# One batch's k^T v steps half a unit later, and one expert's row gathers after the first results

## The chip, the cores and the metric

The kernel runs on one core of a Trainium2 chip. A core has five engines with a queue of instructions each: TensorE (PE; its weight loads are listed as PEld) multiplies matrices into PSUM, VectorE (DVE) and ScalarE (ACT) work on rows, GpSimd (POOL) does small vector work and issues the indirect DMAs, SyncE (SP) issues plain DMAs. Engines wait for each other through semaphores. The metric is the device time of one execution in microseconds (us), and a lower time is better.

## The reference

The computation is linear attention followed by a mixture of experts. The 8 batches have 576 tokens and 8 heads of 64 columns each.

```python
kv = np.einsum('bhsd,bhse->bhde', k, v)
out = np.einsum('bhsd,bhde->bhse', q, kv)
rms = np.sqrt(np.mean(out * out, axis=-1, keepdims=True) + 1e-06)
x = (out / rms * g_norm)              # then (B,H,S,D) -> (4608, 512)
do_compute = x @ w_skip > 0           # the other tokens are passed through
logits = xc @ w_gate                  # xc: the computed tokens; 8 experts
e_idx = np.argmax(logits, axis=1)     # gate_w: softmax at e_idx
h = np.maximum(xc[mask] @ w1[e], 0.0) # 512 -> 1024, tokens of expert e
y[mask] = gate_w[mask, None] * (h @ w2[e])
out[do_compute] = xc + y
```

## The kernel before

Everything is written in one order by hand; the framework adds the semaphores from what the instructions read and write, but moves nothing.

**Attention.** A *unit* `n` is the work on two tiles of 128 tokens for four of the eight heads, and there are 36 of them. A batch has nine chunks of 64 tokens; two pairs of units (`i` = 0 and 1) take eight of these, so a batch has four units. The ninth chunks, the *last tokens*, of four batches are gathered into a pair of units of their own, for which `i` is `None`: units 16 and 17 for the first four batches, 34 and 35 for the others. The fifth batch (b = 4) begins at unit 18. In step `n` of the main loop come, in this order: `turn(n + 1)` (PE transposes q, L460, ACT copies it), `root(n - 1)` (ACT, L525), the jobs listed under "early", `values(n)` (PE multiplies q with k^T v, L496, or L504 for the last tokens; ACT squares, L510), `norm(n - 1)` (DVE reciprocal L532 and scaling `xl`, L537), `squares(n)` (DVE sum, L518; later units have these two the other way round), then the jobs listed under "pe". The values of a unit go to one of two PSUM buffers `o_ps`, which DVE's `xl` frees. The units with `i` = 0 also copy the last tokens of q aside (L479).

A batch's k^T v is summed on PE in portions (`state`, L379), which are spread over the "pe" slots of earlier steps by the table `portions`. After the last portion ACT copies the sum into the tile `kvd` (L386), and three more jobs follow: the *turn* `state_t` (PE turns k^T v by a product with the identity, L393, ACT copies it to `kvT`, L396), the *gate products* `state_m` (PE multiplies `kvT` with the gate's weights, L402, ACT copies two small blocks, L405) and the *exchange* `state_s` (PE moves the halves to the other partitions, L411, ACT copies them, L415). Their PSUM bank `g_ps` is also that of the ranks (`rank`, L645 to L651), which number the tokens within their expert.

**Experts.** Each expert has a fixed number of slots, in the order of their token counts; r = 0 is the fullest. The x rows were written to `out` in DRAM; `gather_all(r, ...)` fetches an expert's rows to a tile `xg` with one indirect DMA per piece (POOL, L1084), `enter` transposes them (PE, L1093), `layer_1` or `fast_1` and `layer_2` or `fast_2` are the two products (PE, L1112, L1124 and L1192), and `result` adds gate times product to the rows (DVE, L1336) and scatters them into `out` (POOL, L1339). As gathers and scatters touch the same DRAM tensor, a gather waits for all scatters ahead of it in the program to have landed, and a scatter for all gathers ahead of it. `blank` clears unused columns of the next hidden tile (POOL, L1106). The weights come by SP (L336 and L346), when PE has finished with the tile that they replace. Expert 0 has its first 192 rows done early, its `result` for these stands in two pieces before its other work. The tiles `xg` of the other experts have three buffers, so that those of experts 1, 2 and 3 are free from the start.

Two places matter here. In the loop over batches that lists the jobs, with `step` the step after the last portion; for the fifth batch `step` is 16, and for it these are the last lines:

```python
at(step, "early", lambda b=b: state_t(b))
at(step, "pe", lambda b=b: state_m(b))
at(step + 1, "early" if step + 1 == n else "pe", lambda b=b: state_s(b))
```

And the gathers of the first three experts (r = 0, 1, 2), which stand together as soon as the slots' rows are known; in `experts`, each later expert r issues those of r + 2 at its start.

Of the kernel before, what the change touches and what calls it, by code (L numbers as in the profile page):

```python
# [17 lines left out]
def kernel(  # L18
# [117 lines left out]
    def load_q(b):  # L136
        if b < B:
            qts[b] = load(q_pool, "q", q, b)
# [93 lines left out]
    for a in range(2):  # L232
        r = slice(a * 64, (a + 1) * 64)
# [45 lines left out]
    for r, cap in enumerate(ROOMS):  # L279
        pieces, off = [], 0  # L280
# [74 lines left out]
    def own(b, w):  # L355

        return kvds[b % KVD][w * 64:(w + 1) * 64, :, w, w, :]
# [7 lines left out]
    def ends_of(x):  # L365

        ap = [list(d) for d in x.ap]
        assert ap[-1] == [1, PK]
        return bass.AP(x.tensor, x.offset, ap[:-1] + [[PK - G, 2], [1, G]])

    def state(b, some):

        kt, vt = kts[b], vts[b]
        for i in some:
            u, c = divmod(i, C)
            for w in range(2):
                for a in range(2):
                    r = slice(a * 64, (a + 1) * 64)
                    nc.tensor.matmul(  # L379
                        out=sum_ps[w * 64:(w + 1) * 64, a, u, :],  # L380
                        lhsT=kt[r, 2 * u + w, c, :], rhs=vt[r, 2 * u + w, c, :],
                        start=(c == 0), stop=(c == C - 1), skip_group_check=True)
        if some.stop < 2 * C:
            return
        for w in range(2):
            nc.scalar.copy(out=own(b, w)[:, :, G:G + 2 * D].rearrange("p u (a d) -> p a u d", a=2),  # L386
                           in_=sum_ps[w * 64:(w + 1) * 64, :, :, :])

    def state_t(b):
        for u in range(2):  # L390
            for w in range(2):
                r = slice(w * 64, (w + 1) * 64)
                nc.tensor.matmul(out=kvT_ps[:, u, r], lhsT=kvds[b % KVD][:, u, w, w, G:G + 2 * D],  # L393
                                 rhs=ident[:, r], start=True, stop=True)
        kvT = att_pool.tile([P, 2, P], FP32, tag="kvT", name="kvT", bufs=1)
        nc.scalar.copy(out=kvT[:, :, :], in_=kvT_ps)  # L396
        kvTs[b] = kvT

    def state_m(b):
        kvT = kvTs.pop(b)  # L400
        for u in range(2):
            nc.tensor.matmul(out=lg_ps[:, u, :, :, :], lhsT=kvT[:, u, :], rhs=gw_b[:, u, :, :, :],  # L402
                             start=True, stop=True)
        for w in range(2):
            nc.scalar.copy(out=ends_of(own(b, w)), in_=lg_ps[w * 64:(w + 1) * 64, :, :, w, :])  # L405

    def state_s(b):

        for w in range(2):
            r, o = slice(w * 64, (w + 1) * 64), slice((1 - w) * 64, (2 - w) * 64)  # L410
            nc.tensor.matmul(out=sw_ps[o, :], lhsT=ident[r, r], rhs=own(b, w), start=True, stop=True,  # L411
                             skip_group_check=True)
        for w in range(2):
            o = slice((1 - w) * 64, (2 - w) * 64)
            nc.scalar.copy(out=kvds[b % KVD][o, :, w, 1 - w, :],  # L415
                           in_=sw_ps[o, :].rearrange("p (u k) -> p u k", u=2))


    units = []
# [22 lines left out]
    def at(step, part, job):  # L442
        todo.setdefault((step, part), []).append(job)
# [470 lines left out]
    for b, n in starts.items():  # L914
        if b:
            step, counts = portions[b]
            i = 0
            for count in counts:
                at(step, "pe", lambda b=b, some=range(i, i + count): state(b, some))
                i += count  # L920
                step += 1
            assert i == 2 * C and step < n and step - len(counts) > over - 1
            at(step, "early", lambda b=b: state_t(b))
            at(step, "pe", lambda b=b: state_m(b))
            at(step + 1, "early" if step + 1 == n else "pe", lambda b=b: state_s(b))
            over = step
        at(over, "end", lambda b=b: load_kv(b + 3))

        at(n + 2, "end", lambda b=b: load_q(b + 2))
# [61 lines left out]
    with tc.tile_pool(name="wpool_b", bufs=1, reuse_waits="tile") as wpool_b, \  # L991
# [384 lines left out]
        def gather_all(r, pieces, src, asrc):  # L1376
            if r < E:
                xgs[r] = xg0 if r == 0 else gather_pool.tile([P, CK, DM], FP32, tag="xg", name="xg",
                                                             bufs=3)
                for piece in pieces[r]:  # L1380
                    gather_piece(xgs[r], piece, src, asrc)

        def experts(pieces, widths, srcs, xt, ht, yps0, tables, group):

            for r in range(E):
                load_ahead(r)
                if yps0 is not None and r == E - 1:
                    nc.gpsimd.drain()
                if r:
                    gather_all(r + 2, pieces, *srcs)  # L1390
                todo = pieces[r]
                end = widths[r]
                new = {}

                def enter(some):
                    for piece in some:
                        expert_in(xgs[r + 1], new["xt"], piece)

                more = pieces[r + 1] if r + 1 < E else []
                if more:  # L1400
                    new["xt"] = new_xt()
                beside = []
                if r == 0:
                    if yps0 is not None:
                        tables = first_tables(lambda fs: layer_1(r, xt, ht, slice(KEPT, end), fs),
                                              tables)
                        result(first[0], yps0[0], xgs[0], tables, group)
                    else:
                        layer_1(r, xt, ht, slice(0, end), range(FC))
                    enter(more[0:1])  # L1410
                    if yps0 is not None:
                        tables = again_gates(tables)
                        result(first[1], yps0[1], xgs[0], tables, group)
                    do(w1_sums(r + 1))
                    enter(more[1:])
                else:
                    fast_1(r, xt, ht, end // 2, w2_sums(r), lambda: enter(more[0:1]))
                    enter(more[1:])
                if more:
                    n = widths[r + 1] // 2  # L1420
                    beside = x_sums(r + 1, new["xt"], n) + (w1_sums(r + 1) if r else [])
                if r == 0:
                    if yps0 is None:
                        gather_all(2, pieces, *srcs)
                    ys = [bank() for _ in todo]
                    for fs in (range(HF), range(HF, FC)):
                        for piece, y in zip(todo, ys):
                            layer_2(r, ht, piece, y, fs)
                    do(beside, 4)
                    for piece, y in zip(todo, ys):  # L1430
                        result(piece, y, xgs[r], tables, group)
                    do(beside)
                else:
                    if yps0 is not None and r == 1:
                        rnd_i = rounds()
                    if yps0 is not None and r == E - 1:
                        n_rounds.append(nc.values_load(rnd_i[0:1, 0:1], min_val=1,
                                                       max_val=ROUNDS + 1))
                    of = {piece[0:2]: piece for piece in todo}
                    part = None  # L1440
                    if yps0 is not None and r == 1:
                        two = half_rows(tables[0][0])
                    if yps0 is not None and r == E - 1:
                        part = lambda c, half, y: half_result(c, half, y, xgs[r], two,
                                                              tables[0][1], group)
                    fast_2(r, ht, todo[2:], beside,
                           lambda key, y: result(of[key], y, xgs[r], tables, group), part)
                del w_sb[r]
                if more:
                    xt, ht = new["xt"], new_ht()  # L1450
                    if yps0 is not None:
                        blank(ht, r + 1)
# [45 lines left out]
        layer_2(0, ht_of, first[0], y, range(3, 4))  # L1498
        again_rows(arows, asrc, range(SOON, len(runs)))
        layer_2(0, ht_of, first[0], y, range(4, FC))  # L1500
        for r in range(3):
            gather_all(r, plan, src, asrc)
        gates()
        layer_2(0, ht_of, first[1], y_more, range(IN, 5))
# [2 lines left out]
        yps0 = [y, layer_2(0, ht_of, first[1], y_more, range(5, FC))]  # L1507
# [74 lines left out]
```

## Time and profile before

| | us |
|---|---|
| median of 3 runs | 381.81 (381.4 to 382.44) |
| the profiled execution | 381.81 |
| its span, first to last instruction | 380.0 |
| busy in the span: PE / PEld / DVE / ACT / POOL | 365.3 / 313.2 / 245.1 / 142.3 / 124.2 |
| PE busy from 57 to 73 | 15.10 of 16.00 |
| PE busy from 142 to 158 | 14.67 of 16.00 |
| PE busy from 158 to 220 | 62.00 of 62.00 |

Times in the trace count from the start of the span. A row of a timeline gives start, duration, engine, line, operation, output<-inputs, shape and how many rows it merges; in brackets stand the idle time before it and what ended it. One float32 matmul of the program leaves two rows of PE. A row of PE that overlaps the next is normal, as matmuls are pipelined, so steps are measured from start to start. Busy time of PE says that it had work in flight and not that it ran at its peak.

### The profile page before, as it was taken

What the parts mean: (1) busy time and instruction counts of PE and PEld (TensorE: products, weight loads), DVE (VectorE), ACT (ScalarE), POOL (GpSimd) and SP (SyncE); (2) the same over time, 40 slices, a digit from 0 to 9 for tenths busy, and PEclk for the clock granted to TensorE, in tenths of its full rate; (3) what the DMA queues carried; (4) which work ended last, traced back from release to release, by engine and by line L of the source; (5) the groups of instructions that cost most, each with busy time, mean ns of one, the idle gap of its engine ahead of it and who ended that gap; (6) DMA issues with size and microseconds to landing.
All of it is one profiled execution on the core that took longest, in us unless ns stands there. A gap on an engine that the chain in (4) does not pass through costs nothing.

```text
span 380.0 us, 9623 instructions
## 1 busy us (share of the span) xinstructions
PE 365.3 (96%) x3848; PEld 313.2 (82%) x3848; DVE 245.1 (64%) x626; ACT 142.3 (37%) x383; POOL 124.2 (33%) x195
## 2 busy tenths in 40 slices
PE   8999999999988998999999999999999999999994
PEld 4688797898977857779869987988988998998983
DVE  3344458667787961666756665875876876877831
ACT  2366676676774301214402430430440430431410
POOL 7025467655668544223013302212201211202003
PEclk9999999999999999999999999999999999999999
DMA  8999999996487738966516462672662762800001
GB/s 292 393 390 389 403 402 398 403 352 205 136 296 207 216 92 281 394 203 237 194 62 201 144 223 57 232 257 68 239 213 87 261 194 92 273 3 28 29 1 52
DMA packets 32039, 81.70 MB, mean 215 GB/s; under 512 B 2474, under 2 KB 2482, under 8 KB 31988
## 3 DMA queue, kind: packets, MB, share of 16 engines
q1 hardware_dynamic: 28176, 69.47, 52.1%
q0 software_dynamic: 3792, 11.53, 8.9%
q8 instruction: 32, 0.52, 0.6%
q14 instruction: 19, 0.16, 0.1%
q10 hardware_dynamic: 20, 0.02, 0.0%
HBM read 66.80 MB, written 14.48 MB: 214 GB/s over the span
## 4 chain that ended last, share of the span: by engine, by line
PE 84%; issue 6%; DVE 3%; ACT 3%; POOL 2%; DMA 1%; POOLq 0%; DVEq 0%; ACTq 0%
PE bank L1192 44%; PE bank L1124 9%; PE o_ps L496 6%; PE sum_ps L379 5%; PE bank L1112 4%; PE q_ps L460 3%; PE g_ps L393 2%; PE q_ps L170 2%; PE bank L1093 2%; DMA xg<-out_dram,src 1%; DVE rs L518 1%; DVE xl L537 1%; ACT sq L510 1%; PE q_ps L814 1%; PE g_ps L411 1%
## 5 line engine op out<-in xcount | busy, mean ns | idle before, releaser
L1202 ACT COPY p<-bank 128x128 f32<-128x128 f32 (+6 forms) x70 | 20.8, 297 | 100.3 <-PE bank L1192 89.3
L1192 PE MATMUL bank<-xt,w 128*128 128x128 f32 (+5 forms) x336 | 55.5, 288 | 0.1
L567 POOL TENSOR_TENSOR xb<-xl,g_b 128x512 f32<-128x512 f32 x36 | 44.4, 1234 | 32.5 <-DVE rs L532 30.6
L1192 PEld LDWEIGHTS bank<-xt,w 128*128 128x128 f32 x336 | 47.0, 190 | 2.0 <-DVE bank L1196 1.5
L1196 DVE TENSOR_TENSOR bank<-bank,p 128x128 f32<-128x128 f32 (+6 forms) x70 | 23.6, 337 | 37.1 <-PE bank L1192 36.0
L1192 PE MATMUL bank<-xs,s 128*128 128x128 f32 (+5 forms) x224 | 36.7, 289 | 0.0
L496 PE MATMUL o_ps<-kvd,qT 128*128 128x146 f32 x240 | 35.8, 290 | 1.0 <-ACT kvd L415 0.7
L1339 POOL DMA_INDIRECT out_dram<-xg,arows x9 | 10.0, 1112 | 78.7 <-DVE xg L1336 77.8
L518 DVE TENSOR_REDUCE rs<-sq 128x8 f32<-128x512 f32 x36 | 24.6, 682 | 16.2 <-ACT sq L510 16.0
L1124 PE MATMUL bank<-w,ht 128*32 128x128 f32 (+2 forms) x436 | 34.5, 319 | 0.0
L496 PEld LDWEIGHTS o_ps<-kvd,qT 128*128 128x128 f32 x240 | 31.6, 188 | 2.0 <-ACT kvd L415 1.5
L1192 PEld LDWEIGHTS bank<-xs,s 128*128 128x128 f32 x224 | 31.1, 190 | 1.0 <-ACT p L1202 0.8
L1339 POOL DMA_INDIRECT out_dram<-xg,rows x14 | 13.9, 994 | 53.2 <-DVE xg L1336 42.7
L1124 PEld LDWEIGHTS bank<-w,ht 128*32 128x32 f32 (+2 forms) x436 | 18.8, 120 | 13.2 <-issue 10.9
L537 DVE TENSOR_TENSOR xl<-o_ps,rs 128x584 f32<-128x584 f32 x34 | 26.1, 767 | 4.5 <-DVE rs L532 0.5
L1192 PE MATMUL bank<-t,ht 128*128 128x256 f32 x112 | 27.1, 385 | 0.0
L1192 PE MATMUL bank<-w,ht 128*128 128x256 f32 x112 | 27.1, 384 | 0.0
L1084 POOL DMA_INDIRECT xg<-out_dram,src x14 | 14.4, 1026 | 37.2 <-DMA out_dram<-xg,rows 13.9
L379 PE MATMUL sum_ps<-v,k 64*64 64x64 f32 x1152 | 25.6, 228 | 0.6 <-issue 0.6
L510 ACT ACTIVATE sq<-o_ps 128x512 f32<-128x512 f32 x34 | 20.3, 596 | 15.0 <-PE o_ps L496 14.5
L379 PEld LDWEIGHTS sum_ps<-v,k 64*64 64x64 f32 x1152 | 21.7, 140 | 4.7 <-issue 2.1
L1192 PE MATMUL bank<-t,hs 128*128 128x256 f32 x112 | 25.3, 379 | 0.0
(217 smaller groups left out, 680.5 us busy)
## 6 DMA issues: line engine op xcount, KB each, us to landing
w<-in_moe_w_dram SPq DMA_DIRECT2D x16, 2048.0 KB, 7.9
k<-in_k_dram SPq DMA_DIRECT2D x16, 576.0 KB, 9.7
v<-in_v_dram SPq DMA_DIRECT2D x16, 576.0 KB, 12.0
q<-in_q_dram SPq DMA_DIRECT2D x16, 576.0 KB, 9.2
out_dram<-xb SPq DMA_DIRECT2D x29, 256.0 KB, 4.4
out_dram<-xb POOLq DMA_DIRECT2D x7, 256.0 KB, 5.5
xg<-out_dram,src POOLq DMA_INDIRECT x16, 3.5
out_dram<-xg,rows POOLq DMA_INDIRECT x16, 7.1
```

Of the source, the lines that this page charges most:

```text
L379: nc.tensor.matmul(out=sum_ps[w * 64:(w + 1) * 64, a, u, :], lhsT=kt[r, 2 * u + w, c, :], rhs=vt[r, 2 * u + w, c, :], start=(c == 0), stop ...
L496: nc.tensor.matmul(out=ps[:, w, 0:2 * PK].rearrange("p (r k) -> p r k", r=2)[:, :, cols], lhsT=qT[:, w, a, :], rhs=kvds[b % KVD][:, u, w, ...
L510: nc.scalar.activation(out=sq[:, :, :, :], in_=heads(ps, G, G + 2 * D), func=ACT.Square)
L518: nc.vector.tensor_reduce(out=rs[:, :, :], in_=sq[:, :, :, :].rearrange("p x y (a d) -> p x (y a) d", a=2), axis=AX.X, op=ALU.add)
L537: nc.vector.tensor_tensor(out=xl[:, :, :, :].rearrange("p x y (a k) -> p x (y a) k", a=2), in0=ps[:, :, 0:2 * PK].rearrange("p x (h k) -> ...
L567: late.append((lambda: nc.gpsimd.tensor_tensor(out=xb[:, :, 4 * u * D:(4 * u + 4) * D].rearrange("p r (w x) -> p r w x", w=2), in0=xl[:, : ...
L1112: nc.tensor.matmul(out=hps[:, cols], lhsT=w_sb[r][0][:, dc, f * P:(f + 1) * P], rhs=xt[:, dc, cols], start=(dc == 0), stop=(dc == DC - 1))
L1124: nc.tensor.matmul(out=yps[q * m:(q + 1) * m, 0:n], lhsT=ht(f)[:, off:off + m], rhs=w_sb[r][1][:, f, q * n:(q + 1) * n], start=(f == 0), s ...
L1192: nc.tensor.matmul(out=out, lhsT=lhsT(i), rhs=rhs(i), start=start and i == 0, stop=i == k - 1, skip_group_check=True)
L1196: nc.vector.tensor_tensor(out=to, in0=x, in1=y, op=ALU.add)
L1202: nc.scalar.copy(out=t, in_=x)
L1339: ins = nc.gpsimd.indirect_dma_start(out=cut_rows(m)[:, :], out_offset=bass.IndirectOffsetOnAxis(ap=rows[:, col:col + 1], axis=0), in_=x, ...
```

## The change

Two edits, independent of each other. First: where the step after a batch's last portion has a unit of last tokens (`bare`), the turn is listed under "pe", behind that step's values, instead of "early", before them; the gate products move to the next step's "pe" slot, and the exchange from there to the step after that, which for the fifth batch is the step of its own first unit, under "early". Of all batches the fifth alone has such a step. Second: the three gathers of expert r = 2 leave the place where those of 0 and 1 are issued, and go to `experts`, after the two early results of expert 0 and after the rows of expert 1 have been transposed, ahead of expert 0's second layer. In the code after the change all lines behind the first edit are numbered three higher (L1093 becomes L1096), two higher at the end.

```diff
-            at(step, "early", lambda b=b: state_t(b))
-            at(step, "pe", lambda b=b: state_m(b))
-            at(step + 1, "early" if step + 1 == n else "pe", lambda b=b: state_s(b))
+            bare = units[step][2] is None
+            at(step, "pe" if bare else "early", lambda b=b: state_t(b))
+            at(step + bare, "pe", lambda b=b: state_m(b))
+            ready = step + bare + 1
+            assert ready <= n
+            at(ready, "early" if ready == n else "pe", lambda b=b: state_s(b))
...
                 if r == 0:
-                    if yps0 is None:
-                        gather_all(2, pieces, *srcs)
+                    gather_all(2, pieces, *srcs)
                     ys = [bank() for _ in todo]
...
-        for r in range(3):
+        for r in range(2):
             gather_all(r, plan, src, asrc)
```

## The prediction, made before the changed kernel was run

> **What bounds the kernel now.** I read the page first, then the windows by stage, the chain, and last the timelines of the two places that the diff touches. TensorE is busy nearly everywhere and runs at full clock:
>
> ```profile
> PE 365.3 (96%) x3848; PEld 313.2 (82%) x3848; DVE 245.1 (64%) x626; ACT 142.3 (37%) x383; POOL 124.2 (33%) x195
> PE 84%; issue 6%; DVE 3%; ACT 3%; POOL 2%; DMA 1%; POOLq 0%; DVEq 0%; ACTq 0%
> 57.00:73.00 16.00, 15.10 (x336) 13.04 (x332) 11.76 (x30) 10.21 (x27) 11.07 (x21) 1.00 1.05 401
> 142.00:158.00 16.00, 14.67 (x142) 13.03 (x141) 4.68 (x11) 3.98 (x13) 5.42 (x6) 1.00 0.93 316
> ```
>
> The last two rows are windows (start:end, length, then busy time of PE, its weight loads, DVE, ACT and POOL, clock, DMA share, GB/s). In the stretch of the first edit PE idles 16.00 - 15.10 = 0.90 us, in that of the second 1.33 us. That caps what either can win; only new waits can cost more. The timelines of PE around the fifth batch's turn, and around the third batch's exchange, which stands where the new one will:
>
> ```profile
> 63.55 0.58 PE L379 MATMUL sum_ps<-v,k 64*64 64x64 f32 x24
> 64.71 1.19 PE L393 MATMUL g_ps<-ident,kvd 128*128 128x64 f32 x8 [0.59 <-ACT kvd L386]
> 65.83 0.74 PE L504 MATMUL o_ps<-kvd,q 64*64 64x73 f32 x32
> 66.50 0.64 PE L402 MATMUL g_ps<-gw_b,kvT 128*128 128x36 f32 x4
> ...
> 42.16 0.66 PE L460 MATMUL q_ps<-ident,q 128*128 128x128 f32 x4
> 42.74 0.71 PE L411 MATMUL g_ps<-kvd,ident 64*64 64x292 f32 x4
> 43.38 0.41 PE L479 MATMUL o_ps<-ident,q 128*64 128x128 f32 x2
> 44.11 1.27 PE L496 MATMUL o_ps<-kvd,qT 128*128 128x146 f32 x8 [0.32 <-ACT kvd L415]
> ```
>
> See the 0.59 us before L393: the turn waits for ScalarE's copies of the sum. And see that where the exchange (L411) comes right before the values (L496), PE waits 0.32 us for the exchange's copies. POOL in the second place, and PE's first use of the third expert's rows:
>
> ```profile
> 144.53 0.94 POOL L1084 DMA_INDIRECT xg<-out_dram,src  x1 [0.30 <-issue]
> 145.78 0.95 POOL L1084 DMA_INDIRECT xg<-out_dram,src  x1 [0.30 <-issue]
> 147.03 0.95 POOL L1084 DMA_INDIRECT xg<-out_dram,asrc  x1 [0.30 <-issue]
> 157.34 1.03 POOL L1339 DMA_INDIRECT out_dram<-xg,rows  x1 [9.36 <-DVE agate L1523]
> 158.67 1.01 POOL L1339 DMA_INDIRECT out_dram<-xg,arows  x1 [0.30 <-issue]
> 166.81 0.98 POOL L1339 DMA_INDIRECT out_dram<-xg,arows  x1 [7.13 <-DVE xg L1336]
> 168.10 0.98 POOL L1339 DMA_INDIRECT out_dram<-xg,arows  x1 [0.30 <-issue]
> 176.39 1.30 POOL L1084 DMA_INDIRECT xg<-out_dram,src  x1 [7.14 <-DMA out_dram<-xg,arows]
> ...
> 182.86 0.60 PE L1093 MATMUL bank<-ident,xg 128*128 128x128 f32 x4
> ```
>
> The first three are the third expert's gathers; the last POOL row is the fourth expert's, which waited until the four scatters before it had landed: 176.39 - 168.10 = 8.3 us after the last was issued.
>
> **First edit: the fifth batch's steps.** No instruction is added or dropped; the turn is four matmuls (eight rows) and one ACT copy, the gate products two and two, the exchange two and two. No DMA goes with them. PE's order from 63.55 on becomes: sum, values 16, turn (L393), sum, ranks (L645 to L651), query turn 18, values 17, gate products (L402), sum, query turn 19, exchange (L411), L479, values 18, sum. I lay it from PE's own starts, each the distance from one start to the next:
> - Values 16 no longer wait for the turn but for their buffer, freed by DVE's xl of unit 14 (63.59 + 0.77 = 64.36). Unit 15's values started 0.14 after such an end (62.24, 62.38): 64.50.
> - Values 16 take 0.67 (65.83 to 66.50): 65.17. The copies (64.21 + 0.75 = 64.96) are done, so the 0.59 is gone.
> - Turn: 1.12 before, with a short wait for the second copy; 0.85 busy for the first batch's eight, which wait for nothing. I take 0.98: 66.15.
> - Sum, 24 rows, 0.58: 66.73. The ranks share g_ps with the turn and must let the kvT copy finish (0.1 + 0.37 after the turn, about 66.65): no wait. Ranks 0.70 (67.70 to 68.40): 67.43. Query turn 0.57: 68.00.
> - Values 17, followed by L402 as values 16 were, 0.67: 68.67. L402 0.56 (66.50 to 67.06): 69.23. It now waits for DVE's reads of the ranks (0.5 us after them before, so about 68.0): covered. Sum of 16 rows, about 0.40 from 0.58 for 24 and 0.75 for 40: 69.63.
> - From query turn to values behind an exchange: 1.95 in the third batch (42.16 to 44.11). On ACT the exchange's copies queue behind the query copy and the root. What waits there is L496, and behind it on PE the next sum, on ACT the squares of unit 18. Values 18: 71.58. They then take 1.20 (44.11 to 45.31) as they wait for the second copy too: the next sum starts at 72.78.
>
> Before, that sum starts at 72.36. So the edit moves a wait instead of removing it and **costs 0.42 us**: about 0.7 won at the turn, about 1.1 lost at the exchange, which today overlaps the sum of 16 rows (L411 and L379 together 0.83, from 69.53 to 70.36, so 0.43 for L411; apart 0.64, 42.74 to 43.38, + 0.40). Lower end: values 16 right behind the sum (-0.37), turn at 0.85 (-0.13), no wait for the copies (-0.32, and 0.11 for the second): -0.5. Upper end: turn still 1.12 (+0.14), the second batch's 2.08 (28.97 to 31.05) instead of 1.95 (+0.13), ranks held by the kvT copy (+0.2): +0.9. I stay at 0.42, as the third batch's rows are the same sequence. The delay reaches the end: in 73 to 118 us PE is busy 41.72 of 45.00 and its waits there start from PE's own results.
>
> [...]
>
> **Second edit: the third expert's gathers.** Taken from 144.53, they free 3 x (0.95 + 0.30) = 3.75 us of POOL, which then idles until 157.34 anyway: nothing. They free 320 rows x 2 KB = 0.66 MB from a DMA that runs at 316 GB/s in that window, some 2 us of loads landing earlier. No wait of PE there names a DMA (0.60 and 0.49 issue, 0.24 DVE gate), so I take 0; bounds -1.33 and 0.
>
> Put behind the first two scatters, they must wait for these to land, since they read the same tensor. Second scatter 158.67 + 8.3 = 167.0; three gathers at 1.30, 0.97 and 0.94 with 0.30 between end at 170.8, the last issued at 169.9. Gathers land 2.6, 3.4 or 9.9 us (least, median, most) after issue: 173.3, at worst 179.8. PE wants them at 182.86, or 183.3 with the first edit: 3 to 10 us to spare, cost 0. Behind them on POOL: the first expert's two other scatters (166.81 before) go out at 173.3 to 179.8; the blanking of the second expert's hidden tile (169.07) slips to 176 to 182, read first at 197.41 by L1124; the fourth expert's gathers (176.39) slip to 183 to 190, wanted at 218.40. The second expert's scatters (196.37) wait for those to land, at worst 200; nothing on PE waits for a scatter but the fifth expert's gathers, wanted at 249.00. On SP nothing moves: its weight loads (154.32, 166.82, 184.07) wait for PE. All of this is covered by PE's 26.00 of 26.00 busy us in 158 to 184 and 36.00 of 36.00 in 184 to 220.
>
> [...]
>
> **Sum.** 0.42 + 0 on the profiled execution's 381.81 (span 380.0 and 1.8 around it), which is also the median of the three: **382.2 us**, 0.1% slower. A measurement here tells about 0.3% (1.15 us) from no change.
>
> **Rivals.**
> [...]
> - *The early gathers were in PE's way* (faster). If the 1.33 us idle in 142 to 158 came from them, 381.81 + 0.42 - 1.33 = 380.9. Against: no such releaser.
> - *The first edit does what it is named for*: the wait is won, the exchange's is hidden: its lower end, 381.3.
> - *It costs its upper end or more*, as values 19 and ScalarE's squares slip too: 382.7 to 383.2.
>
> **Numbers.** Forecast 0.53 (own range 381.6 to 382.8), late gathers 0.19, early gathers in the way 0.11, edit works 0.07, edit dearer 0.10. Slower by over 0.3% is most of the late gathers, half of the dearer edit and the forecast's edge: 0.30. Faster by over 0.3% lies at the far side of the second rival: 0.12. Within: 0.58. The range takes in 380.9 and half of the late gathers: 380.9 to 383.8.
>
> **What would show it.** Right: no wait at L393 near 65, L496 of unit 18 with a wait for kvd L415 of about 0.3 and the sum at about 72.8; the gathers near 165 to 171 with a wait for the scatters; L1093 (then L1096) near 183 without a wait. Wrong: a PE wait for DMA xg there, a next sum before 72.3, or a PE busy time that changes in 118 to 356.

## The result, and the profile after

The changed kernel takes 384.08 us in the median of 22 runs (381.8 to 385.93), the kernel before 381.73 in 22 runs beside it: a ratio of 1.0066, interval 1.0051 to 1.0082, so 0.7% slower. Forecast was 382.2 with a range up to 383.8. Its profiled execution took 384.66 us with a span of 382.9.

The page of the changed kernel and its windows by stage (start:end, length, busy time of PE, weight loads, DVE, ACT, POOL, granted clock, DMA share, GB/s):

```profile
PE 367.1 (96%) x3848; PEld 314.7 (82%) x3848; DVE 243.7 (64%) x626; ACT 143.1 (37%) x383; POOL 124.0 (32%) x195
...
57.00:73.00 16.00, 15.05 (x307) 12.59 (x307) 12.05 (x30) 10.21 (x25) 12.04 (x21) 1.00 1.04 400
118.00:142.00 24.00, 23.41 (x184) 18.66 (x185) 16.57 (x49) 5.57 (x13) 11.93 (x20) 0.93 0.60 176
142.00:158.00 16.00, 15.77 (x149) 13.18 (x149) 6.01 (x13) 3.77 (x11) 4.12 (x5) 1.00 0.88 305
158.00:184.00 26.00, 24.24 (x184) 19.20 (x183) 17.66 (x38) 6.85 (x20) 7.39 (x8) 1.00 0.64 219
```

The stage of the first edit has hardly changed. The other three have: from 118 to 142 the clock was 0.93 (1.00 before), from 142 to 158 PE is busier than before (15.77 against 14.67), and from 158 to 184, where the prediction had counted on 26.00 of 26.00, PE idles 1.76 us.

The first edit's place, PE's timeline after:

```profile
63.88 0.58 PE L379 MATMUL sum_ps<-v,k 64*64 64x64 f32 x24
64.83 0.74 PE L504 MATMUL o_ps<-kvd,q 64*64 64x73 f32 x32 [0.37 <-DVE xl L537]
65.51 1.10 PE L393 MATMUL g_ps<-ident,kvd 128*128 128x64 f32 x8
...
70.56 0.71 PE L411 MATMUL g_ps<-kvd,ident 64*64 64x292 f32 x4
71.20 0.41 PE L479 MATMUL o_ps<-ident,q 128*64 128x128 f32 x2
71.93 1.27 PE L496 MATMUL o_ps<-kvd,qT 128*128 128x146 f32 x8 [0.32 <-ACT kvd L415]
73.13 0.93 PE L379 MATMUL sum_ps<-v,k 64*64 64x64 f32 x48
```

From sum to sum it takes 73.13 - 63.88 = 9.25 us, before 72.36 - 63.55 = 8.81: the edit costs 0.44. The wait at L393 is gone, and a wait of 0.32 stands at L496.

The values of the last unit and the first products of expert 0's rows, in the kernel before and after:

```profile
117.38 0.74 PE L504 MATMUL o_ps<-kvd,q 64*64 64x73 f32 x32 [1.44 <-DVE xl L537]
118.56 2.87 PE L814 MATMUL q_ps<-xt_first,w 128*128 128x192 f32 x16 [0.44 <-ACT xt_first L830]
121.27 0.98 PE L1112 MATMUL bank<-xt_first,w 128*128 128x192 f32 x5
```

```profile
118.15 0.74 PE L504 MATMUL o_ps<-kvd,q 64*64 64x73 f32 x32 [1.43 <-DVE xl L537]
119.33 4.55 PE L814 MATMUL q_ps<-xt_first,w 128*128 128x192 f32 x16 [0.44 <-ACT xt_first L830]
123.72 1.46 PE L1115 MATMUL bank<-xt_first,w 128*128 128x192 f32 x8
```

The same sixteen rows take 4.55 us instead of 2.87, and the next product begins 1.68 us later against them. In both profiles the granted clock changes on a raster of 3.41 us. The changed kernel's records have 1.00 from 10.34 to 119.57, 0.50 to 122.98 and 1.00 to 382.39: stretches of 109.23, 3.41 and 259.41 us, which are 32, 1 and 76 times the one of 3.41. Before, they have 1.00 from 10.44 to 379.08, 368.64 us or 108 times, and 0.50 from there. Windows cut on each run's raster, before and after:

```profile
116.26:119.67 3.41, 1.85 (x39) 1.70 (x40) 3.03 (x8) 1.84 (x5) 3.25 (x7) 1.00 0.96 230
119.67:123.08 3.41, 3.41 (x23) 3.41 (x22) 2.42 (x6) 1.10 (x3) 2.83 (x8) 1.00 1.02 292
```

```profile
116.16:119.57 3.41, 1.53 (x47) 1.06 (x40) 2.90 (x6) 1.84 (x6) 3.23 (x7) 1.00 0.82 187
119.57:122.98 3.41, 3.41 (x12) 3.41 (x12) 3.03 (x7) 0.51 (x2) 2.99 (x8) 0.50 0.99 297
```

After, PE worked 1.53 of 3.41 us, and the granted clock of the next 3.41 us was 0.50. Before, the raster lay otherwise over the same work: PE worked 1.85 of such a stretch, and the clock stayed.

The second edit's place. Before, PE's first products of expert 1 had no wait:

```profile
166.69 0.85 PE L1192 MATMUL bank<-xt,w 128*128 128x172 f32 x4
167.38 1.45 PE L1192 MATMUL bank<-xs,s 128*128 128x172 f32 x8
```

After: the same products and the turning of expert 2's rows, then POOL, and then what DVE, ACT and SP did at the wait:

```profile
167.74 0.85 PE L1195 MATMUL bank<-xt,w 128*128 128x172 f32 x4
168.43 0.75 PE L1195 MATMUL bank<-xs,s 128*128 128x172 f32 x4
170.93 0.85 PE L1195 MATMUL bank<-xs,s 128*128 128x172 f32 x4 [1.76 <-ACT p L1205]
...
185.81 0.60 PE L1096 MATMUL bank<-ident,xg 128*128 128x128 f32 x4
...
166.94 0.99 POOL L1087 DMA_INDIRECT xg<-out_dram,src  x1 [6.83 <-DMA out_dram<-xg,arows]
168.24 0.97 POOL L1087 DMA_INDIRECT xg<-out_dram,src  x1 [0.30 <-issue]
169.51 0.95 POOL L1087 DMA_INDIRECT xg<-out_dram,asrc  x1 [0.30 <-issue]
177.85 1.02 POOL L1342 DMA_INDIRECT out_dram<-xg,arows  x1 [7.39 <-DVE bank L1199]
...
169.78 0.35 DVE L1339 SCALAR_TENSOR_TENSOR xg<-bank,agate,xg 128x128 f32<-128x128 f32 x1 [2.19 <-PE bank L1195]
...
170.58 0.30 ACT L1205 COPY p<-bank 128x172 f32<-128x172 f32 x1 [11.11 <-issue]
...
169.78 0.37 SPq L346 DMA_DIRECT2D w<-in_moe_w_dram  x1
```

The gathers run as forecast and their rows are turned (L1096) without a wait. But PE stops for 1.76 us at expert 1's third product. It waits for ACT's copy `p`, which needs the first product, and that ended in the records at about 167.74 + 0.85 = 168.59. The copy began at 170.58, 1.99 later. The DVE operation and the weight load that wait for the product before it both began at 169.78, some 2 us after PE's record of its end. So PE's results reached three engines late, while POOL issued the three gathers. The trace also keeps the semaphore updates: the one that DVE and SP waited for came at 169.76, ACT's at 170.51, so the results were late before these engines could act on them.

Where the 2.9 us between the spans are: 0.33 ahead of 63.88; 0.44 in the first edit; 1.68 in the halved clock; 1.40 won between 121.27 and expert 1's first product (166.69 - 121.27 = 45.42 before, 167.74 - 123.72 = 44.02 after); 1.85 lost from there to the end (380.0 - 166.69 = 213.31, 382.9 - 167.74 = 215.16). Sum 2.90.

The mean clocks of the 22 runs say how often a stretch was lost, though not where. One had a clock of 1.0 and took 381.8, twelve had 0.994 or 0.995, five 0.993 and four 0.988 to 0.990, these with 384.33 to 385.93 us. One halved stretch of 3.41 us is 0.0045 of the span's clock.

### The profile page after: what moved, and what is told of

Read it like the earlier page. It is cut to its first block, busy times and chain, and to the rows that moved or that the text cites. A ratio compares the mean times of both kernels' runs of the same rounds, so it can differ in the third digit from the quotient of the medians.

```text
span 382.9 us, 9626 instructions
## 1 busy us (share of the span) xinstructions
PE 367.1 (96%) x3848; PEld 314.7 (82%) x3848; DVE 243.7 (64%) x626; ACT 143.1 (37%) x383; POOL 124.0 (32%) x195
## 4 chain that ended last, share of the span: by engine, by line
PE 81%; issue 9%; DVE 3%; ACT 3%; POOL 2%; DMA 1%; POOLq 0%; DVEq 0%; ACTq 0%
PE bank L1195 43%; PE bank L1127 7%; PE o_ps L496 6%; PE sum_ps L379 5%; PE bank L1115 4%; PE q_ps L460 3%; PE g_ps L393 2%; PE q_ps L170 2%; PE bank L1096 2%; PE q_ps L814 1%; DMA xg<-out_dram,src 1%; DVE rs L518 1%; DVE xl L537 1%; ACT qT L463 1%; PE g_ps L402 1%
## 5 line engine op out<-in xcount | busy, mean ns | idle before, releaser
L567 POOL TENSOR_TENSOR xb<-xl,g_b 128x512 f32<-128x512 f32 x36 | 43.5, 1212 | 33.4 <-DVE rs L532 31.5
L496 PE MATMUL o_ps<-kvd,qT 128*128 128x146 f32 x240 | 35.9, 290 | 1.3 <-ACT kvd L415 1.0
L496 PEld LDWEIGHTS o_ps<-kvd,qT 128*128 128x128 f32 x240 | 31.6, 188 | 2.6 <-ACT kvd L415 2.1
```

The source lines that it names most:

```text
L496: nc.tensor.matmul(out=ps[:, w, 0:2 * PK].rearrange("p (r k) -> p r k", r=2)[:, :, cols], lhsT=qT[:, w, a, :], rhs=kvds[b % KVD][:, u, w, ...
L567: late.append((lambda: nc.gpsimd.tensor_tensor(out=xb[:, :, 4 * u * D:(4 * u + 4) * D].rearrange("p r (w x) -> p r w x", w=2), in0=xl[:, : ...
```

## The experiments

They ran in four groups, the kernel before beside each: the first group on one chip, the second on another, the third and fourth both on a third. The kernel before differs by chip (380.23, 380.03, 382.24 and 381.67 us), so everything is compared within its group. "Stretch lost" counts the runs whose mean clock is 0.995 or less; a stretch lost at the start of a run counts too.

| group | kernel | us | ratio to before (95%) | stretch lost |
|---|---|---|---|---|
| 1 | before | 380.23 | | 19 of 33 |
| 1 | first edit alone | 380.67 | 1.0017 (0.9996 to 1.0038) | 8 of 12 |
| 1 | second edit alone | 379.98 | 0.9996 (0.9976 to 1.0017) | 6 of 12 |
| 1 | before, shifted by 0.9 | 381.65 | 1.0038 (1.0019 to 1.0058) | 11 of 12 |
| 1 | before, shifted by 2.2 | 381.62 | 1.0048 (1.0023 to 1.0073) | 2 of 10 |
| 2 | before | 380.03 | | 17 of 29 |
| 2 | both edits | 380.63 | 1.0015 (0.9993 to 1.0036) | 9 of 12 |
| 2 | both, filled | 379.49 | 0.9991 (0.9970 to 1.0012) | 2 of 12 |
| 2 | before, filled | 379.24 | 0.9981 (0.9964 to 0.9999) | 2 of 12 |
| 3 | before | 382.24 | | 18 of 29 |
| 3 | first, filled | 380.86 | 0.9970 (0.9951 to 0.9989) | 2 of 12 |
| 3 | second, filled | 383.69 | 1.0035 (1.0015 to 1.0054) | 9 of 12 |
| 3 | before, filled | 381.43 | 0.9982 (0.9967 to 0.9998) | 2 of 12 |
| 3 | both edits | 384.63 | 1.0057 (1.0037 to 1.0078) | 6 of 6 |
| 4 | before | 381.67 | | 19 of 34 |
| 4 | gathers beside layer 2, filled | 380.67 | 0.9960 (0.9939 to 0.9980) | 2 of 12 |
| 4 | gathers behind the results, filled | 381.32 | 0.9996 (0.9971 to 1.0020) | 3 of 12 |
| 4 | second, filled | 384.57 | 1.0053 (1.0028 to 1.0079) | 9 of 11; a twelfth run took 925.18 us and is left out |
| 4 | before, filled | 381.07 | 0.9975 (0.9957 to 0.9994) | 1 of 12 |

The ratios are not those of the two medians. They differ most in group 4: by the medians the second edit, filled, is at 1.0076, and the gathers beside layer 2 at 0.9974.

**Group 1: each edit alone, and a plain shift.** The first two are the diff of the change, cut to one edit each. The shifted kernels add to the kernel before, with `fill(8)` and `fill(20)`:

```diff
+    def fill(count):
+        for _ in range(count):
+            nc.tensor.matmul(out=g_ps[:, 0:256], lhsT=ones[:, :],
+                             rhs=ones[:, :].unsqueeze(1).to_broadcast([P, 2, P]), start=True, stop=True,
+                             skip_group_check=True)
...
+    at(18, "pe", lambda: fill(8))
```

> The kernel before with the first edit alone; the nine gathers stay together as before. Known from the changed kernel's profile: the sum that follows the exchange starts 0.77 us later than before (0.33 of it was there before the edit's place, 0.44 is the edit's), everything up to 119.33 keeps that shift, and the granted clock is 0.50 from 119.57 to 122.98, where the same products take 4.55 instead of 2.87 us. Theory A, the first edit's small shift moves the two idle stretches of PE (1.43 and 0.44 us, which both kernels have) into one stretch of 3.41 us in which PE is then busy for under half, and the clock is halved for the next such stretch: clock of about 0.994, 383.6 to 384.4 us in most runs, with the 0.50 near 120 in the profile. Theory B, the clock's drop comes from the second edit or from chance: clock 0.999 and 382.2 us (the edit's 0.44 alone).

> The kernel before with the second edit alone: expert 2's three gathers are issued after the early results. Theory A (the clock drop belongs to the first edit's shift): the clock stays at 0.999; against before, 1.1 to 1.4 us are won between 143 and 150, where the copies and ReLUs of ACT no longer come late, and 1.76 us are lost at the first product of expert 1 near 168, where DVE, ACT and the weights' DMA get PE's results late while the gathers are issued: 381.8 to 382.4 us. Theory B (the second edit is what costs): 383.5 us or more, with a clock of 0.995. The prediction's own sum gave this edit 0: 381.8 us, without a wait near 168.

> The kernel before with neither edit, and eight products without use added to PE after the values of unit 18, estimated at 0.85 us from the 0.43 us of the program's warm-up products with twice the columns at half the clock. Theory A (the place of the idle stretches against the 3.41 us raster of the clock decides): the idle stretches of 1.44 and 0.44 us come to lie at 116.8 to 118.2 and 119.0 to 119.4, inside the same raster stretch 116.26 to 119.67 as in the changed kernel, so the clock drops to 0.5 for 3.41 us near 120: 381.8 + 0.85 + 1.7 = 384.3 us, clock about 0.994. Theory B (the clock drop needs the edits themselves): 382.6 us, clock 0.999.

> The same with twenty such products, an estimated 2.1 us, two and a half times the delay of the run with eight. Theory A: the stretch of 1.44 us then lies at 118.0 to 119.5 in the raster stretch up to 119.67 and that of 0.44 behind it, so PE is busy for 0.58 of the one and more of the next: no drop, clock 0.999, 381.8 + 2.1 = 383.9 us, less than or the same as with eight products. Theory B: also 383.9, but then 1.3 above the run with eight; theory A puts the two runs within 0.5 us of each other.

Neither edit alone costs what both had cost together, and on this chip the second costs nothing. Sum to sum the first edit alone took 72.44 - 63.20 = 9.24, the second alone 71.79 - 62.98 = 8.81: 0.43 for the first edit again. In its profile the stretch 116.10 to 119.52 had PE busy for 1.80 and the next kept clock 1.00, so theory A's stretch near 120 was not lost in that run. The second edit alone shows no wait at expert 1's start on this chip, though POOL issues the gathers at the same place (164.34 to 167.98):

```profile
164.68 0.85 PE L1192 MATMUL bank<-xt,w 128*128 128x172 f32 x4
165.37 1.45 PE L1192 MATMUL bank<-xs,s 128*128 128x172 f32 x8
```

Its clock of 0.993 is a stretch lost from 7.13 to 10.54, at the start. The shifted kernels had added 0.88 and 2.19 us in their profiles. By their medians both cost the same, 1.4 us, although one has 1.3 us more to do (by the ratios 1.4 and 1.8, with intervals that overlap): the smaller shift lost a stretch in eleven of twelve runs, the larger in two of ten. Windows of the smaller shift, then of the larger:

```profile
114.68:118.10 3.42, 1.70 (x66) 1.23 (x62) 2.55 (x6) 1.85 (x6) 3.02 (x7) 1.00 0.67 147
118.10:121.51 3.41, 3.29 (x10) 3.29 (x11) 3.03 (x7) 0.87 (x3) 3.09 (x8) 0.50 0.92 307
```

```profile
114.13:117.54 3.41, 2.02 (x42) 1.51 (x40) 2.38 (x5) 2.04 (x5) 3.09 (x5) 1.00 0.51 95
117.54:120.95 3.41, 2.96 (x46) 2.81 (x47) 3.03 (x7) 1.36 (x4) 3.25 (x7) 1.00 0.87 265
```

So a shift with neither edit in it acts through the clock. That both came out 2.3 to 2.7 us below the forecast in absolute terms is put down to the chip, on which the kernel before is 1.5 us faster and itself loses a stretch in over half of its runs.

**Group 2: the idle stretch filled.** To the changed kernel and to the kernel before, the same `fill` is added with

```diff
+    at(NU - 1, "early", lambda: fill(10))
```

where PE waits 1.4 us for DVE before the last unit's values.

> The changed kernel itself again, beside the next three on one chip. On the chip of the first four experiments the two edits cost 0.44 (interval -0.15 to 1.4) and -0.25 (-0.9 to 0.65) us one by one, where together they had cost 2.5 us. Theory A (the halved clock is a matter of where the idle stretches fall in the raster, and so of the chance of each run, on which small shifts act): on a chip where the kernel before also loses a clock stretch in half of its runs, both edits together cost 0 to 1 us. Theory B (the edits cost 2.5 us only together): ratio 1.005 to 1.008 here as well.

> The changed kernel, with ten products without use (estimated 1.1 us, from 0.88 us for eight) on PE in the idle stretch of 1.4 us ahead of the values of the last unit. Theory A (too little work of PE within one raster stretch halves the next): no run shows the 0.50 near 120, the clock of all runs is that of the start and the end alone (0.996 or more), and the time is 1.0 to 1.7 us below the changed kernel's on the same chip, although PE has more to do. Theory B (the clock drop has another cause, or the idle time is not it): same clock, same time as the changed kernel or up to 0.3 us more.

> The kernel before with the same ten products in the same idle stretch. Theory A: where the kernel before loses a clock stretch in half of its runs (19 of 33 had a clock of 0.992 to 0.994 on the chip of the first experiments), it wins 0.5 to 1.0 us in the median and its slowest runs come nearer; where it never loses one, the time stays the same within 0.2 us. Theory B: the same time or up to 0.3 us more.

> The kernel before unchanged, for its profile on this chip. In the profile that the prediction was made from, ACT's copy of the turned rows began 1.35 us after the end of the products it waits for (143.78) and its next ReLU 3.66 us after (149.52), while the gathers of experts 1 and 2 were issued, and the first product of expert 1 found no wait; in the second edit alone on another chip nothing of this kind was seen at 142 to 150 or at 164 to 168. If these late results belong to the gathers, they are here again; if they belong to the chip or the run, they can be missing.

The filler shows in the changed kernel's windows as PE time where none was, and no stretch is lost near 120:

```profile
113.04:116.45 3.41, 3.03 (x78) 2.33 (x76) 2.27 (x5) 1.59 (x4) 2.93 (x8) 1.00 0.63 129
116.45:119.86 3.41, 3.00 (x18) 3.00 (x19) 3.03 (x6) 1.25 (x5) 3.24 (x7) 1.00 0.93 303
```

PE has 1.25 us more to do and the kernel is 1.14 us faster than unfilled; the kernel before gains 0.79. Lost stretches fall from 9 to 2 and from 17 of 29 to 2 of 12. The halved clock near 120 thus came of too little PE work within a stretch: 1.59 of 3.41 us from 115.57 to 118.98 in the unfilled run beside it, followed by 0.50, against the 3.03 above, followed by 1.00. With the clock mostly out of the way the two edits together cost 0.25 us on this chip, less than the two intervals can tell from nothing. Unfilled they cost 0.60 here, within theory A's 0 to 1; the interval (0.9993 to 1.0036) leaves out theory B's 1.005 to 1.008.

The look at the kernel before found nothing late on this chip. ACT's copy began at 140.58 and its ReLUs ran at PE's pace:

```profile
140.58 0.58 ACT L828 COPY xt<-bank 128x512 f32<-128x512 f32 x1 [9.52 <-PE bank L1093]
...
143.34 0.29 ACT L1114 ACTIVATE ht<-bank 128x148 f32<-128x148 f32 x1 [2.01 <-PE bank L1112]
```

From the last unit's values to expert 1's first product it takes 163.41 - 115.49 = 47.92 us; in the profile the prediction was made from, 166.69 - 117.38 = 49.31. So the gathers alone do not make results late; something of the chip or the run has a part in it.

**Group 3: each edit alone, filled.** The same filler in the kernels with one edit each.

> The first edit alone, with the ten products without use in PE's idle stretch of 1.4 us that the filled kernels have. With the halved clock out of the way the edit's own cost is to be seen: the prediction's 0.42 (0.44 in the changed kernel's profile) above the filled kernel before, which was at 0.9981 of the kernel before: ratio about 0.999 to 1.000. A theory in which the edit's shift acts only through the raster would have it equal to the filled kernel before; a theory in which it costs more than its path, 1.002 or more.

> The second edit alone, filled in the same way. The prediction gave it 0: the ratio of the filled kernel before, 0.998 (0.997 to 0.999). If this chip shows PE's results late beside the gathers, as the first chip's two profiles did, the profile has no late copies of ACT at 142 to 150 and a wait of 1 to 2 us at the first product of expert 1, and the sum of the two is -1.4 to +0.4 us; if not, neither is there and the edit is worth 0 within 0.2 us.

> The filled kernel before once more, on the chip of its two filled neighbours, so that these are compared with it: 0.997 to 0.999 of the kernel before, if that loses a clock stretch in half of its runs here too; 1.000 within 0.0005 if it never does.

> The changed kernel on this chip: filled, the two edits together stood 0.25 us above the filled kernel before on the last chip, and unfilled 0.6 us above the kernel before. Expected 1.001 to 1.002 where PE's results come without delay, and 1.005 to 1.008 with waits at 168 where they come late, as on the first chip.

This chip shows late results, and the second edit is what costs: 383.69 against 381.43 for the filled kernel before, 2.26 us. The first edit stands 0.57 below its control with intervals that overlap, so its 0.44 is neither seen nor refuted by these times. Both edits are at 1.0057, near the 1.0066 of the first measurement. The second edit alone in PE's timeline and in windows:

```profile
165.80 0.85 PE L1200 MATMUL bank<-xt,w 128*128 128x172 f32 x4
166.49 0.75 PE L1200 MATMUL bank<-xs,s 128*128 128x172 f32 x4
169.20 0.85 PE L1200 MATMUL bank<-xs,s 128*128 128x172 f32 x4 [1.97 <-ACT p L1210]
```

```profile
166.75:170.16 3.41, 1.44 (x10) 1.18 (x9) 1.33 (x4) 0.68 (x3) 0.95 (x1) 1.00 0.68 196
170.16:173.58 3.42, 3.42 (x14) 3.42 (x13) 1.79 (x4) 0.84 (x3) 1.07 (x2) 0.50 1.00 334
```

The wait comes with a second price: it empties a stretch of PE (1.44 of 3.41), and the next is run at half clock. In the run with both edits two stretches were lost, 119.45 to 122.86 and 170.65 to 174.06, and its clock was 0.988; four of the first 22 runs had 0.988 to 0.990.

**Group 4: the same gathers elsewhere.** On the filled kernel before: one kernel issues expert 2's gathers ahead of the two early scatters, tied to copies of the row numbers that DVE makes after the gate sums; one puts them behind expert 0's last results.

```diff
+                        late = [slot_pool.tile([P, x.shape[1]], I32, tag="late%d" % i, name="late%d" % i)
+                                for i, x in enumerate(srcs)]
+                        for to, x in zip(late, srcs):
+                            nc.vector.tensor_copy(out=to[:, :], in_=x[:, :])
+                        gather_all(2, pieces, *late)
                         result(first[0], yps0[0], xgs[0], tables, group)
...
-        for r in range(3):
+        for r in range(2):
             gather_all(r, plan, src, asrc)
```

```diff
                     for piece, y in zip(todo, ys):
                         result(piece, y, xgs[r], tables, group)
+                    if yps0 is not None:
+                        gather_all(2, pieces, *srcs)
                     do(beside)
...
-        for r in range(3):
+        for r in range(2):
             gather_all(r, plan, src, asrc)
```

> The filled kernel before, with expert 2's three gathers tied to copies of their row numbers that DVE makes behind the gate sums, so that they are issued from about 155.5 to 159.5, ahead of the two early scatters, while PE multiplies expert 0's rest for 8 us and needs nothing of ACT. Theory A (PE's results reach the others late while gathers are issued, on some chips): no wait at expert 1's first product, no late ReLUs at 149; on a chip that shows late results, 1.0 us less than the filled kernel before; on one that doesn't, the same within 0.2 us. Theory B (the place decides, whatever is issued): a wait of 1.5 us or more at expert 1's first product here too.

> The filled kernel before, with the three gathers behind expert 0's last two results: they wait for these scatters to land and are issued at about 173 to 177, their rows wanted by PE at 182. Theory A: no wait at expert 1's first product near 167 on any chip; at 173 to 177 ACT's copies beside PE's products of expert 1 come late on a chip that shows late results, which costs 0.5 to 1.5 us there, against 1.0 won at 142 to 150. Theory B: the wait near 167 stays. On a chip without late results: the same as the filled kernel before within 0.2 us.

> The second edit alone, filled, again: on a chip with late results 1.003 to 1.005 of the kernel before, with a wait of about 2 us at expert 1's first product and a clock of 0.50 behind it; on one without, 0.998 to 0.999 and no such wait.

> The filled kernel before, as the control of the three others: 0.997 to 0.999 of the kernel before; on a chip with late results its copies of ACT at 142 to 150 are late and PE waits 0.4 to 0.6 us twice there.

The wait at expert 1's start is there with the gathers and gone without them, so the place alone does not make it. The repeated second edit has it again (2.07 us, then a lost stretch, 1.0053). The kernel with the gathers beside layer 2 has none at expert 1's start, although POOL issues four scatters there (165.87 to 170.79); its PE, and then its POOL:

```profile
165.57 0.85 PE L1200 MATMUL bank<-xt,w 128*128 128x172 f32 x4
166.25 1.45 PE L1200 MATMUL bank<-xs,s 128*128 128x172 f32 x8
...
155.25 0.94 POOL L1092 DMA_INDIRECT xg<-out_dram,late  x1 [11.46 <-issue]
156.50 1.37 POOL L1092 DMA_INDIRECT xg<-out_dram,late  x1 [0.30 <-issue]
158.17 0.94 POOL L1092 DMA_INDIRECT xg<-out_dram,late  x1 [0.30 <-issue]
```

It is the fastest kernel of this chip: 0.9960 of the kernel before, where the changed kernel stood at 1.0057 in the third group. Against its control it gained 0.40 us where 1.0 was expected, with overlapping intervals, so that its own gain is not shown by the times; in the profiles it is 0.86 from the last unit's values to expert 1 (116.94 to 165.57 against 115.46 to 164.95). In the control four ReLUs of ACT came in one burst after 5 us, while PE's products went on, until PE stopped for 0.41 us:

```profile
147.66 0.85 ACT L1122 ACTIVATE ht<-bank 128x148 f32<-128x148 f32 x4 [5.01 <-remote]
```

With the gathers behind the results (175.03 to 178.85) PE has no wait either; the expected loss of 0.5 to 1.5 us there is not in the profile, and the time is 0.25 above the control, within the intervals. Expert 2's rows were turned at 181.49 without a wait. So the wait takes both, the gathers and this place.

## Why the prediction was wrong, by its own steps

The sum was 0.42 + 0. In the profiled run the 0.42 became 0.44, and the 0 became -1.40 and +1.85; a term that the sum did not have, the clock, came to 1.68; 0.33 more lay ahead of both edits.

**First edit, 0.42.** Right. The walk from start to start gave values 17 behind the query turn, a wait of 0.32 at L496 and 1.20 for these values; measured are 0.32 and 73.13 - 71.93 = 1.20. The whole edit is 0.44 here and 0.43 in the profile of the first edit alone. The bounds -0.5 to 0.9 were not needed.

**Second edit, what it removes, taken as 0.** This step failed where results come late. "No wait of PE there names a DMA" was true, and still the way to expert 1 was shorter without the gathers. The two waits marked "issue" and ACT beside them, in the kernel before:

```profile
144.58 4.29 PE L1112 MATMUL bank<-xt,w 128*128 128x148 f32 x32 [0.60 <-issue]
149.46 0.73 PE L710 MATMUL g_ps<-bv,oha_k 128*128 128x72 bf16 x17 [0.49 <-issue]
...
143.78 0.58 ACT L828 COPY xt<-bank 128x512 f32<-128x512 f32 x1 [10.85 <-PE bank L1093]
149.52 0.85 ACT L1114 ACTIVATE ht<-bank 128x148 f32<-128x148 f32 x4 [4.99 <-PE bank L1112]
```

The first wait ends with ACT's late copies. The second ends 0.06 us ahead of ACT's late ReLUs, and 0.06 to 0.08 ahead in three profiles of the third chip, so ACT's ReLUs did not release PE there; what did is not known. In the two first profiles the way to expert 1 is 1.40 us shorter after, all of the 1.33 of the rival "the early gathers were in PE's way". On the third chip, filled, the second edit wins 49.49 - 48.60 = 0.89 us from the last unit's values to expert 1 (control: 115.46 to 164.95; second edit: 117.40 to 166.00); there the first of the two waits stands (0.62). On the other two chips nothing is won there: the way is 47.92 us with it, and 47.91 (first edit alone) and 47.92 (kernel before) without.

**Second edit, what it adds, taken as 0.** This is the step that failed most, the largest term of the profiled run. All that it said of DMAs and POOL holds: gathers issued at 166.94 to 170.46 (forecast 167.0 to 170.8), the rest of the scatters at 177.85, the fourth expert's gathers at 184.34, no wait at L1096. What failed is "covered by PE's 26.00 of 26.00 busy us in 158 to 184". That was read as cover, but at expert 1's start PE needs ACT's copy of the first product before its third, and a result that arrives 2 us late there empties PE. The measured term is 1.76 to 2.07 us of wait (2.41 in the second profile of both edits) and, in three of the four profiles with it, a stretch at half clock behind it, an estimated 1.7 us (3.41 x 0.5). With the gain ahead the medians lie 2.26 and 3.50 us above the two controls on that chip, by the ratios 2.0 and 3.0.

**The clock, not in the sum.** The quoted windows had 1.00 in the clock's column, and the prediction treated it as given. "Only new waits can cost more" failed here: the clock is a term of its own, 1.68 us in the profiled run. PE's idle stretches of 1.43 and 0.44 us near 117 stand in both kernels; a shift of some tenths decides whether both lie within one stretch of the clock's raster. The first edit's delay is such a shift, and so is every run's own start. Which share of the loss near 120 in the first measurement is due to the edit can't be told: on the other chips the kernel before loses a stretch in over half of its runs too. A hint that it seldom did in the first measurement: its 22 runs, whose clocks are not on record, reach 382.44, only 0.63 above the profiled one, which had a clock of 0.999.

**The rivals.** Late gathers had 0.19 of the chances and a part in the range's upper end, but no run shows a cost of theirs: in the changed kernel expert 2's rows were turned at 185.81 without a wait, and the measured 384.08 came about in another way. "A PE busy time that changes in 118 to 356" stood among the signs of a wrong forecast, and it was the right one.

What the runs show of the clock: the records have it at 1.00 or at 0.50, and the drop near 120 lasted one stretch of 3.41 us (119.57 to 122.98). The raster is not tied to the kernel's start: in three runs of the changed kernel the drop began at 119.57, 118.98 and 119.45. Near 117 and 168, 1.35 to 1.70 us of work in 3.41 were followed by 0.50, and 1.80 to 2.02 by 1.00. Busy time is not the whole measure, though: at the start of the second edit alone 2.72 of 3.42 us (3.71 to 7.13) were followed by 0.50 too, and near the end of the kernel with the gathers beside layer 2, 1.45 of 3.41 us (372.04 to 375.45) were followed by 1.00. For the start the 1.00 in the clock's column says little: in the kernel before the column has it from 0 on, but the products without use there (L170) start 0.43 us apart from 1.47 to 4.46 and 0.22 apart from 10.50 to 10.93.

**What stays open.** Why PE's results come late beside gathers on one chip and not on two others was not found. It is not each gather: those at 155 to 159 made nothing late, and beside those at 175 to 183 one ReLU came 0.7 us late (182.39, by the record of a product that ended at 181.65), without a wait of PE. Nor can the records tell whether PE finished late or its results were announced late. ACT's burst of four speaks for the second: in the kernel before the semaphore updates for its products came at 149.50, 149.59, 149.69 and 149.78, where the next ReLUs stand 1.0 us apart. The DVE operation and ACT's copy 0.80 us apart at expert 1's start speak for the first, as they lie 0.79 apart where nothing is late (166.83 and 167.62 in the kernel before). The ends of PE's rows settle neither, as the profile models them. That the first measurement was made on the third chip isn't known; its two profiles show the same late results.

## What to carry to other kernels

An engine that is busy all the time in the profile is not by that alone cover for a transfer's issue moved beside it (PE had 26.00 of 26.00 us, and then a wait of 1.76): look for the hand-overs there that must be answered at once, and move the issue to a stretch in which PE needs no other engine. Lay PE's idle stretches against the raster of 3.41 us on which the clock changed in these runs; where two of them, here of 1.43 and 0.44 us, can fall together, work without use in one of them took 0.6 to 0.8 us off the kernel before. Compare versions with that lottery taken out, and on more than one chip, before an edit is given a gain or a loss of half a percent.

## What was not expected of the hardware

- Near 117, PE idle for 1.9 us in two pieces of one 3.41 us stretch ran the next at half clock, which cost 1.7 us more (4.55 against 2.87 us for the same sixteen rows).
- Adding 1.25 us of products without use made the changed kernel 1.14 us faster, and a delay of 2.2 us cost the same 1.4 us as one of 0.9.
- On one chip of three, and in the two first profiles, PE's results reached ACT, DVE and SP late by some 2 us at expert 1's start (ACT's copy by 1.99 to 2.64), and ACT's ReLU by 3.66 us (149.52 in the kernel before), while gathers were issued or up to 1.5 us behind. On the two other chips the same gathers made nothing late; the kernel before is 1.4 to 2.2 us slower on that chip than on the two others.
